# A fused attention, mixture-of-experts and squared-ReLU kernel: the cost rules by which its attention stage is put in order

## The chip, the cores and the metric

The kernel runs on one core of one Trainium2 chip. Its time is the device time of one execution in microseconds (us). TensorE does the matrix products, VectorE (DVE in the rows), ScalarE (ACT) and GpSimd (POOL) do elementwise work, SyncE (SP) issues most DMAs. Each engine carries out its instructions in the order in which the program lists them, and waits where a semaphore tells it to.

## The reference

Three layers follow one another. Sizes: batch 2, 8 heads, 576 positions, head size 64, so 1152 rows of 512; 4 experts with hidden size 1024; a last layer with hidden size 2048.

```python
# attention with a causal window of 128 and a slope per head
scores = scale * q @ k.T;  scores = where(0 <= rel < 128, scores + bias, -1e9)
attn = exp(scores - max);  attn = attn / (sum(attn) + 1e-9);  o = attn @ v
# every expert on every row, weighted
p = domain_probs / (sum(domain_probs) + 1e-9)
x = sum_e p[:, e] * (relu(o @ w1[e]) @ w2[e])
# last layer
h = relu(x @ w_in);  out = (h * h) @ w_out
```

All of it is float32. The kernel splits most operands into a rounded high part and a remainder ("h" and "l" in its names, as wh and wl, qh and ql, khl, xh and xl), and adds three products.

## The kernel before, in words

From the first microsecond to about 130 us the kernel does attention, and between its steps the first expert's rows: 24 "items" (three column chunks of the rows, 8 hidden blocks each), each a first product (L1031, for the first four L1819), a ReLU, and a second product (L1267, L1770). After that come the fourth chunk, the other experts and the last layer, whose order the program writes out directly.

The first stage's order isn't written by hand. The class `Plan` (L36 to L130) holds a list of tasks, each with the engines that may do it, with an assumed occupation and latency for each, the tasks that it depends on, and a due time. `Plan.run` repeats one step: it works out for each ready task the engine on which it would end first (a later engine of the task's list is taken only if it ends 0.3 us earlier: `OTHER`), finds the earliest start, and among the tasks that could start on that engine within 0.15 us of it (`LOOK`) emits the one with the earliest due time. So the plan fixes which engine does a task and the order of instructions on every engine; the chip's waits then keep the data right, whatever the real durations are.

The plan knows one kind of contention. Tasks marked `shared` (roundings and remainders that read and write SBUF: qh, ql, kh, kl, the first rows' xh and xl, and the weight parts wh and wl) are lengthened when they are put on VectorE while the last GpSimd task is still occupying GpSimd: by what is left of it, up to twice the task's own length. GpSimd tasks are never lengthened.

Attention goes through units (a batch, a pair of heads, up to two query tiles of 128). For each query tile `job_tasks` (L823) adds a chain: scores on TensorE (L868, or L852 for the last 64 rows), the mask on VectorE (L886, L884), bias and maximum on VectorE (L906, L899), exp on ScalarE with the sum (L915), the reciprocal on VectorE (L922, L926), the normalising multiplication `norm` (on GpSimd at L937; only the first tile of a batch, called raw, may also take VectorE, L931), the transposition on TensorE (L948), the copy out of PSUM (L519 or L521), and two triangular masks on GpSimd (L969). Then the product with v (L767) needs the masked tile. There are 32 such norm tasks outside the raw units: 24 with two squares of 128x128 and 8 with one.

The weights of the first expert come in 8 loads. Each becomes a wh (two halves, 128x512, L519 or L521) and a wl (two halves, L525) by `weight_parts` (L1705). The first four loads are used unconverted by the first four items, and their parts, needed again from the second chunk, are the last four in the list `parted` (places j = 4 to 7). For these, places 5 to 7 wait on the second product of the last item of the first chunk and on the remainders of the raw units (L1718).

Of the kernel before, what the change touches and what calls it, by code (L numbers as in the profile page):

```python
# [12 lines left out]
ACTF = mybir.ActivationFunctionType  # L13
# [16 lines left out]
class Buf:  # L30
# [3 lines left out]
    def __init__(self, kind):  # L34
        self.kind, self.users, self.end, self.tile = kind, 0, 0.0, None


class Plan:
# [6 lines left out]
    OTHER = 0.3  # L45
    COLD = 3.0
    WARM = 24.0

    def __init__(self, slots):
        self.tasks = []  # L50
        self.slots = slots
        self.held = {k: [] for k in slots}
        self.at = dict(PE=0.0, ACT=0.0, DVE=0.0, POOL=0.0, SP=0.0)
        self.pool_busy = (0.0, 0.0)

    def add(
        self, name, opts, fn, deps=(), takes=(), bufs=(), due=0.0, follow=(), cold=True,
        shared=False
    ):
        t = dict(  # L60
            name=name, opts=opts, fn=fn, deps=[d for d in deps if d], takes=list(takes),
            bufs=list(takes) + list(bufs), due=due, end=None, follow=[d for d in follow if d],
            cold=cold, shared=shared,
        )
        for b in t["bufs"]:
            b.users += 1
        self.tasks.append(t)
        return t
# [22 lines left out]
    def run(self, until=None):  # L91
        todo = self.tasks
        while todo and not (until and until()):
            cand = []
            for t in todo:
                r = self.ready(t)
                if r is None:
                    continue
                best = None
                for eng, occ, lat in t["opts"]:  # L100
                    start = max(self.at[eng], r)
                    if eng == "PE" and t["cold"] and start < self.COLD:
                        occ, lat = 1.7 * occ, lat + 0.7 * occ
                    if best is None or start + lat + self.OTHER < best[1] + best[3]:
                        best = (eng, start, occ, lat)
                cand.append((best, t))
            assert cand, [t["name"] for t in todo[:20]]
            first, _ = min(cand, key=lambda c: c[0][1])
            eng, start = first[0], first[1]
            (eng, start, occ, lat), t = min(  # L110
                (c for c in cand if c[0][0] == eng and c[0][1] <= start + self.LOOK),
                key=lambda c: c[1]["due"],
            )
            if eng == "DVE" and t["shared"] and self.pool_busy[1] > start:
                more = min(2.0 * occ, self.pool_busy[1] - start)
                occ, lat = occ + more, lat + more
            t["start"], t["end"] = start, start + lat
            self.gap = start - self.at[eng] if start < self.WARM else 0.0
            self.at[eng] = start + occ
            if eng == "POOL":  # L120
                self.pool_busy = (start, start + occ)
            for b in t["takes"]:
                self.held[b.kind].append(b)
            t["fn"](eng)
            for b in t["bufs"]:
                b.users -= 1
                b.end = max(b.end, t["end"])
            todo.remove(t)
# [3 lines left out]
def kernel(  # L132
# [14 lines left out]
    nc = tc.nc  # L147
# [12 lines left out]
    FTQ = FT // NQ  # L160
# [28 lines left out]
    def w_src(e, g, k):  # L189
        if k == 0:  # L190
            return w1s[e][0][:, g * FQ:(g + 1) * FQ].rearrange("(k p) f -> p k f", p=P), KT, FQ
        return w1s[e][1][g * FQ:(g + 1) * FQ, :].rearrange("(k p) d -> p k d", p=P), FTQ, DM
# [14 lines left out]
    def w_tile(shape, dtype, name):  # L207
        i = free.pop(0)
        return wbuf[i].tile(shape, dtype, tag=f"wb{i}", name=name), i
# [321 lines left out]
    def dve(n, lat=0.05):  # L531
        return ("DVE", 0.15 + 0.00105 * n, 0.15 + 0.00105 * n + lat)
# [4 lines left out]
    def pe(us):  # L537
        return ("PE", us, us + 0.25)
# [283 lines left out]
    def job_tasks(u, i, t, add, b_, end, ready, G, q0, k0, pos, wide):  # L822
# [5 lines left out]
        raw = t == 0  # L828
# [4 lines left out]
        rows, squares = (2 * n, 1) if twin else (n, G)  # L833
        s = {k: Buf(k) for k in ("sc", "ts", "st", "tp")}
        m = n if raw else P
# [5 lines left out]
        def stage(name, opts, fn, lag, **kw):  # L841
            mine[name] = add(key + name, opts, fn, due=end - lag - later, follow=[last.get(name)], **kw)
            return mine[name]
# [84 lines left out]
        def norm(eng):  # L928
            ts, st = s["ts"].tile, s["st"].tile
            if eng == "DVE":  # L930
                nc.vector.tensor_tensor(  # L931
                    out=ts[0:rows], in0=ts[0:rows],
                    in1=st[0:rows, 3, 0:squares].unsqueeze(2).to_broadcast([rows, squares, m]), op=ALU.mult,
                )
                return
            for g in range(squares):
                nc.gpsimd.tensor_scalar(  # L937
                    out=ts[0:rows, g, :], in0=ts[0:rows, g, :], scalar1=st[0:rows, 3, g:g + 1],
                    scalar2=1.0, op0=ALU.mult, op1=ALU.mult,
                )  # L940
# [34 lines left out]
        if twin:  # L975
            if "last" not in task:
                task["last"] = plan.add(
                    "last", [("POOL", 2.2, 2.3)], build_last, due=70.0,
                    deps=[task["bias", x, False] for x in range(NP)],
                )  # L980
            tb.append(task["last"])
        us = G * (0.25 if raw else 2 * max(0.107, w * 0.00047))
        tsc = stage("sc", [pe(us)], scores, 7.4, deps=ready,
                    takes=[s["sc"]],
                    bufs=[b_[k] for k in (() if raw else ("qh", "ql", "khl"))])
        if not raw:
            us = 0.15 + 0.00105 * G * n
            tsc = stage("jo", [("DVE", us, us + 0.05)], join, 6.8, deps=[tsc, tb[-1] if twin else t_keep], bufs=[s["sc"]])
        us = G * (0.215 if raw else 0.16 + 0.001 * m)
        tmx = stage("mx", [("DVE", us, us + 0.1)], top, 9.5 if raw else 6.4,  # L990
                    deps=[tsc] + tb, takes=[s["ts"], s["st"]], bufs=[s["sc"]])
        tex = stage("ex", [("ACT", squares * (0.30 + 0.00078 * m), squares * (0.30 + 0.00078 * m) + 0.1)], exp,
                    7.5 if raw else 5.3, deps=[tmx], bufs=[s["ts"], s["st"]])
        tin = stage("in", [("DVE", 0.33, 0.38)], inv, 3.8, deps=[tex], bufs=[s["st"]])
        us = squares * (0.44 if raw else 0.24 + 0.00085 * m)
        tno = stage("no", [("POOL", us, us + 0.05)] + [dve(G * m)] * raw,
                    norm, 3.4, deps=[tin], bufs=[s["ts"], s["st"]])
        ttp = stage("tp", [pe(squares * 0.108)], turn, 2.4, deps=[tno, task["ident"]],
                    takes=[s["tp"]], bufs=[s["ts"]])
        thi = stage("hi", [act(G * n), dve(G * n)], hi, 2.0, deps=[ttp],  # L1000
                    takes=[b_["pt"]] if i == 0 else [], bufs=[s["tp"]] + ([b_["pt"]] if i else []))
        if raw:
            return [thi]
        us = 0.2 + 0.00085 * G * n
        tow = stage("ow", [("POOL", us, us + 0.05)], lambda eng: part(True), 1.6, deps=[thi],
                    bufs=[b_["pt"]])
        tbe = stage("be", [("POOL", us, us + 0.05)], lambda eng: part(False), 1.4, deps=[tow],
                    bufs=[b_["pt"]])
# [425 lines left out]
    PER = 2 * NQ  # L1434
# [191 lines left out]
    for c in range(NP):  # L1626
        for own in (True, False):
# [3 lines left out]
                deps=[t_rel if own else t_join],  # L1631
# [28 lines left out]
    for u in range(len(units)):  # L1660
        if u < NP:
            unit_tasks(u, [14.0 + 2.0 * u])
        else:
            end = 38.0 + 5.5 * (u - NP)
# [4 lines left out]
    RAW1, RAW2 = 4, 4  # L1669
# [16 lines left out]
    def weight_parts(i):  # L1686
        e, g, k = order[i]
        _, nk, nf = w_src(e, g, k)
        parts = (w1t, w2t)[k]
        n = nk // 2  # L1690
        t = wtask["load", i]
        raw = FTQ * g < (RAW1, RAW2)[k]
        later = T0 + (T1 if raw else 0.0) + ITEM * (FTQ * g + (LAG if k else 0))

        def hi(eng, h):
            if h == 0:
                parts[e, g] = [w_tile([P, nk, nf], F32R, name) for name in ("wh", "wl")]
            ks = slice(h * n, (h + 1) * n)
            rounded(eng, parts[e, g][0][0][:, ks, :], wtask["raw", i][:, ks, :])

        def lo(eng, h):
            ks = slice(h * n, (h + 1) * n)
            (wh, _), (wl, _) = parts[e, g]
            rest(eng, wl[:, ks, :], wtask["raw", i][:, ks, :], wh[:, ks, :])
            if h == 1:  # L1705
                ready.add(i)
                if raw:
                    raw_done(i)
                else:
                    free.append(raws.pop(i)[0][1])  # L1710

        m = n * nf

        j = parted.index(i)
        room_ = [task["pv", NP - 1]] if j else []
        if j > 1:
            room_ += [wtask["lo", parted[j - 2], 1], wtask.get(("used", parted[j - 2]))]
        if raw and j > PER - (RAW1 + RAW2) // FTQ:  # L1718
            room_ += [itask["g2", FT - 1]] + [task["evl", u] for u in range(NP)]
        for h in range(2):  # L1720
            a = wtask["hi", i, h] = plan.add(
                f"wh{i}.{h}", [act(m), dve(m)], lambda eng, h=h: hi(eng, h),
                shared=True, deps=[t] + room_, due=later - 4.0 + h,
                follow=[wtask.get(("hi", i, 0))],
            )
            wtask["lo", i, h] = plan.add(
                f"wlo{i}.{h}", [gps(m), dve(m)], lambda eng, h=h: lo(eng, h),
                shared=True, deps=[a], due=later - 3.0 + h, follow=[wtask.get(("lo", i, 0))],
            )
# [163 lines left out]
    for i in range(PER):  # L1893
        weight_load(i)
    t_pt = plan.add("pt", [("SP", 0.6, 6.0)], lambda eng: nc.sync.dma_start(
        out=pt, in_=probs.rearrange("(t p) e -> p t e", p=P)
# [41 lines left out]
    for it, (e, ch, f, two) in list(enumerate(items))[N1:]:  # L1938
# [4 lines left out]
        g = f if two else f // FTQ  # L1943
# [66 lines left out]
```

## Time and profile before

| what | value |
|---|---|
| time, median of 3 runs | 647.51 us (647.49 to 647.77) |
| the profiled execution | 648.88 us |
| its span, first to last instruction | 646.9 us |
| TensorE busy in the span | 636.7 us (98%) |
| mean granted clock of TensorE | 0.997 |

The span is what the profile's rows lie in; the execution adds 2.0 us around it. TensorE's rows are pipelined: a row's length is its latency, and the steps between the starts of rows say how fast they go.

### The profile page before, as it was taken

The page shows a single profiled execution, that of the slowest core. Times are in us where ns is not written, and L with a number is a line of the kernel's source. Part 1 is how long each engine was busy: PE and PEld are TensorE (multiplying, and loading weights), DVE is VectorE, ACT ScalarE, POOL GpSimd, SP SyncE. Part 2 cuts the span into 40 slices and gives each one's busy share as a digit, 9 for nine tenths or more (in the row PEclk, how much of TensorE's full clock was granted, in tenths as well). Part 3 has the DMA queues.
Part 4 walks back from the last instruction along what each step waited for, and adds up shares of the span by engine and source line. Part 5 has one row for each costly group of instructions (what it writes and reads, how often), then busy time and mean ns, then how long its engine had stood idle before and what let it go on. Part 6 is the DMA issues. An engine that isn't in the chain of part 4 may idle for free.

```text
span 646.9 us, 11077 instructions
## 1 busy us (share of the span) xinstructions
PE 636.7 (98%) x3929; PEld 570.4 (88%) x3929; DVE 467.4 (72%) x1019; ACT 295.4 (46%) x744; POOL 393.0 (61%) x520
## 2 busy tenths in 40 slices
PE   9999999999999999999999999999999999999997
PEld 8767888899889999899899899899989899898996
DVE  6867967358887877876876876857777667767553
ACT  6867855334444444434434344346554543343230
POOL 2698977339784564565556546247786685665521
PEclk9989999999999999999999999999999999999999
DMA  9953341124125254354443443421114223001012
GB/s 231 275 144 84 81 106 47 39 93 131 34 65 163 82 143 151 93 157 126 119 142 114 130 131 115 130 83 66 33 41 157 81 83 114 16 2 50 1 65 82
DMA packets 46983, 64.70 MB, mean 100 GB/s; under 512 B 6480, under 2 KB 29264, under 8 KB 46928
## 3 DMA queue, kind: packets, MB, share of 16 engines
q1 hardware_dynamic: 35520, 39.48, 20.8%
q10 hardware_dynamic: 11408, 24.51, 12.9%
q8 instruction: 31, 0.51, 0.3%
q14 instruction: 24, 0.20, 0.1%
HBM read 53.23 MB, written 10.75 MB: 99 GB/s over the span
## 4 chain that ended last, share of the span: by engine, by line
PE 94%; POOL 3%; ACT 1%; issue 1%; DMA 0%; DVE 0%; POOLq 0%
PE yacc L1241 38%; PE hps L1150 35%; PE hps L1031 6%; PE yacc L1267 6%; PE sc L868 2%; PE xps L767 1%; PE tp L948 1%; PE hps L1819 1%; POOL ts L937 1%; PE sc L549 1%; POOL pt L969 1%; PE yacc L1770 1%; PE xtp L1333 1%; POOL ql L525 1%; ACT ts L915 0%
## 5 line engine op out<-in xcount | busy, mean ns | idle before, releaser
L1241 PE MATMUL yacc<-wh,hmem 128*128 128x512 f32 x716 | 227.8, 390 | 0.0
L1241 PEld LDWEIGHTS yacc<-wh,hmem 128*128 128x128 f32 x716 | 134.4, 188 | 27.1
L1241 PE MATMUL yacc<-wl,hmem 128*128 128x512 f32 x358 | 139.6, 390 | 0.0
L525 POOL TENSOR_TENSOR wl<-wraw,wh 128x256 fp32r<-128x256 f32 (+1 forms) x80 | 74.7, 958 | 40.8 <-ACT wh L458 29.1
L525 POOL TENSOR_TENSOR hmem<-c,hmem 128x320 fp32r<-128x320 f32 (+1 forms) x64 | 59.2, 943 | 60.3 <-ACT hmem L1181 60.3
L525 POOL TENSOR_TENSOR ls<-wsum,hs 128x256 fp32r<-128x256 f32 x77 | 61.5, 825 | 54.3 <-ACT hs L403 53.6
L1165 DVE TENSOR_TENSOR u<-hps,p 128x256 f32<-128x256 f32 (+1 forms) x80 | 36.4, 455 | 65.2 <-PE hps L1150 63.3
L1161 ACT ACTIVATE p<-hps 128x256 f32<-128x256 f32 (+1 forms) x80 | 32.8, 410 | 108.1 <-PE hps L1150 108.0
L1241 PEld LDWEIGHTS yacc<-wl,hmem 128*128 128x128 f32 x358 | 67.3, 188 | 12.5
L525 POOL TENSOR_TENSOR la<-wraw,ha 128x256 fp32r<-128x256 f32 x54 | 48.6, 919 | 16.8 <-ACT ha L389 16.8
L296 DVE SCALAR_TENSOR_TENSOR wconv<-wraw,wconv 128x512 int32<-128x512 int32 x64 | 57.6, 899 | 1.3
L1185 ACT ACTIVATE hmem<-c 128x256 fp32r<-128x256 f32 (+1 forms) x72 | 31.3, 445 | 53.4 <-DVE c L1165 51.8
L1186 DVE SCALAR_TENSOR_TENSOR hmem<-c,hmem 128x256 fp32r<-128x256 f32 (+1 forms) x72 | 43.3, 623 | 14.0 <-ACT hmem L1185 12.7
L1181 ACT ACTIVATE hmem<-c 128x320 fp32r<-128x320 f32 (+1 forms) x64 | 27.3, 446 | 52.3 <-DVE c L1175 33.5
L1150 PE MATMUL hps<-ht,ls 128*128 128x320 f32 (+1 forms) x160 | 47.5, 297 | 1.3 <-POOL ls L525 1.3
L1150 PE MATMUL hps<-xh,hs 128*128 128x320 f32 (+1 forms) x160 | 47.6, 297 | 0.0
L1150 PE MATMUL hps<-ht,hs 128*128 128x320 f32 (+1 forms) x160 | 47.5, 297 | 0.0
L1150 PE MATMUL hps<-xl,hs 128*128 128x320 f32 (+1 forms) x160 | 47.4, 296 | 0.0
L1150 PE MATMUL hps<-xh,la 128*128 128x320 f32 (+1 forms) x160 | 47.4, 296 | 0.0
L1150 PE MATMUL hps<-lt,hs 128*128 128x320 f32 (+1 forms) x160 | 47.3, 296 | 0.0
L1150 PE MATMUL hps<-xl,ha 128*128 128x320 f32 (+1 forms) x160 | 47.3, 296 | 0.0
L1150 PE MATMUL hps<-xh,ls 128*128 128x320 f32 (+1 forms) x160 | 47.3, 296 | 0.0
(162 smaller groups left out, 1643.6 us busy)
## 6 DMA issues: line engine op xcount, KB each, us to landing
wraw<-in_w_dram SPq DMA_DIRECT2D x32, 512.0 KB, 3.9
wraw<-in_w_out_dram ACTq DMA_DIRECT2D x16, 512.0 KB, 3.9
w<-wconv ACTq DMA_DIRECT2D x32, 256.0 KB, 4.1
wraw<-w SPq DMA_DIRECT2D x16, 512.0 KB, 3.8
wraw<-in_w_in_dram ACTq DMA_DIRECT2D x14, 512.0 KB, 4.1
rq<-in_qT_dram SPq DMA_DIRECT2D x8, 256.0 KB, 7.4
out_dram<-y SPq DMA_DIRECT2D x7, 256.0 KB, 2.1
rk<-in_kT_dram SPq DMA_DIRECT2D x8, 192.0 KB, 4.9
```

The costliest lines, as they stand in the source:

```text
L296: nc.vector.scalar_tensor_tensor(out=ai, in0=raw[j][:, :, part], scalar=amount, in1=ai, op0=op, op1=ALU.bitwise_or,)
L525: e.tensor_tensor(out=out, in0=in0, in1=f32(in1), op=ALU.subtract)
L868: nc.tensor.matmul(out=sc[0:n, g, :], lhsT=ql[:, qs], rhs=b_["khl"].tile[:, g, j0:j0 + w], start=(ql is b_["qh"].tile), stop=(ql is b_["ql ...
L1031: nc.tensor.matmul(out=ps, lhsT=l_[:, k, cs], rhs=r_[:, k, cols], start=(k == 0 and r_ is xh and l_ is wh and not second), stop=(k == KT - ...
L1150: nc.tensor.matmul(out=ps, lhsT=a[l_][:, k, :], rhs=b[r_][:, k, :], start=start and k == 0 and l_ == r_, stop=stop and k == 1 and l_ == 1, ...
L1161: nc.scalar.activation(out=out, in_=x, func=ACTF.Copy)
L1165: nc.vector.tensor_tensor(out=out, in0=x, in1=y, op=ALU.add)
L1181: nc.scalar.activation(out=hh, in_=r, func=ACTF.Copy)
L1185: nc.scalar.activation(out=hh, in_=src, func=ACTF.Relu)
L1186: nc.vector.scalar_tensor_tensor(out=hl, in0=src, scalar=0.0, in1=f32(hh), op0=ALU.max, op1=ALU.subtract)
L1241: nc.tensor.matmul(out=y, lhsT=l_[:, ns], rhs=r_[:, fo, cols], start=(first and fo == 0 and j == 0), stop=(last and fo == FTQ - 1 and j == 2),
L1267: nc.tensor.matmul(out=y, lhsT=l_[:, ns], rhs=r_[:, fo, :], start=(first and j == 0), stop=(last and j == 2),)
```

## The change

`Plan` keeps for each of GpSimd and VectorE the last task that may hold what both use: on GpSimd every task, on VectorE a `shared` one. When a GpSimd task starts while the kept VectorE task is still running, 0.65 (`HELD`) of what is left of it is added to the GpSimd task. When a `shared` VectorE task starts while the kept GpSimd task is running, 0.3 (`SLOWED`) of the overlap is added to the VectorE task, and 0.65 of the overlap to the GpSimd task, whose end and whose engine's free time move out. The choice of an engine is still made before anything is added.

The norm tasks outside the raw units get ScalarE as a second engine, assumed at 0.22 us a square, as one activation a square (Copy, with the reciprocal as the scale).

Of the parts of the raw weights, only the last place (j = 7) still waits on the last item of the first chunk; places 5 and 6 don't.

```diff
+    HELD = 0.65
+    SLOWED = 0.3
...
-        self.pool_busy = (0.0, 0.0)
+        self.port = dict(POOL=None, DVE=None)
...
-            if eng == "DVE" and t["shared"] and self.pool_busy[1] > start:
-                more = min(2.0 * occ, self.pool_busy[1] - start)
+            other = self.port["POOL" if eng == "DVE" else "DVE"]
+            if other and (eng == "POOL" or eng == "DVE" and t["shared"]):
+                end = other["start"] + other["occ"]
+                if eng == "POOL":
+                    more = self.HELD * max(end - start, 0.0)
+                else:
+                    both = min(occ, max(end - start, 0.0))
+                    more = self.SLOWED * both
+                    other["occ"] += self.HELD * both
+                    other["end"] += self.HELD * both
+                    self.at["POOL"] = max(self.at["POOL"], other["start"] + other["occ"])
                 occ, lat = occ + more, lat + more
-            t["start"], t["end"] = start, start + lat
+            t["start"], t["end"], t["occ"] = start, start + lat, occ
...
-            if eng == "POOL":
-                self.pool_busy = (start, start + occ)
+            if eng == "POOL" or eng == "DVE" and t["shared"]:
+                self.port[eng] = t
...
+            if eng == "ACT":
+                for g in range(squares):
+                    nc.scalar.activation(
+                        out=ts[0:rows, g, :], in_=ts[0:rows, g, :], func=ACTF.Copy,
+                        scale=st[0:rows, 3, g:g + 1],
+                    )
+                return
...
-        tno = stage("no", [("POOL", us, us + 0.05)] + [dve(G * m)] * raw,
-                    norm, 3.4, deps=[tin], bufs=[s["ts"], s["st"]])
+        us_act = squares * 0.22
+        tno = stage("no", [("POOL", us, us + 0.05)] + (
+            [dve(G * m)] if raw else [("ACT", us_act, us_act + 0.1)]
+        ), norm, 3.4, deps=[tin], bufs=[s["ts"], s["st"]])
...
-        if raw and j > PER - (RAW1 + RAW2) // FTQ:
+        if raw and j > PER - (RAW1 + RAW2) // FTQ + 2:
```

## Rows read from the trace of the kernel before

**Rows 1.** The page's first part: busy us, share of the span, instructions.
```profile
PE 636.7 (98%) x3929; PEld 570.4 (88%) x3929; DVE 467.4 (72%) x1019; ACT 295.4 (46%) x744; POOL 393.0 (61%) x520
```
**Rows 2.** Busy time by stage: stretch, its length, engines' busy us (instructions), granted clock, DMA.
```profile
24.00:95.00 71.00, 67.31 (x470) 54.89 (x469) 53.85 (x197) 50.68 (x159) 64.26 (x105) 0.98 0.49 127
95.00:130.00 35.00, 34.89 (x276) 31.39 (x276) 18.18 (x78) 15.71 (x53) 17.90 (x40) 1.00 0.18 53
130.00:647.00 517.00, 512.00 (x2983) 464.14 (x2981) 378.00 (x667) 211.61 (x473) 304.20 (x359) 1.00 0.30 93
```
**Rows 3.** TensorE's waits, 17 to 130 us: us in total, times, longest.
```profile
PE tp L948 <- POOL ts L937: 3.5, 5, 1.0
```
**Rows 4.** The view by stage again, in stretches of 1 us.
```profile
42.00:43.00 1.00, 0.11 (x1) 0.11 (x1) 0.93 (x4) 0.50 (x2) 1.00 (x2) 1.00 0.97 273
43.00:44.00 1.00, 0.44 (x3) 0.25 (x3) 1.00 (x2) 0.00 (x0) 1.00 (x2) 0.92 0.51 176
44.00:45.00 1.00, 1.00 (x6) 1.00 (x6) 0.17 (x1) 0.73 (x2) 1.00 (x2) 0.50 0.82 228
47.00:48.00 1.00, 1.00 (x7) 0.79 (x6) 0.43 (x1) 0.42 (x2) 0.34 (x1) 0.87 0.31 103
```
**Rows 5.** Timeline of GpSimd: start, us, instruction.
```profile
33.43 2.01 POOL L525 TENSOR_TENSOR ql<-rq,qh 128x512 fp32r<-128x512 f32 x1
36.10 1.28 POOL L525 TENSOR_TENSOR wl<-wraw,wh 128x512 fp32r<-128x512 f32 x1
40.52 1.26 POOL L525 TENSOR_TENSOR wl<-wraw,wh 128x512 fp32r<-128x512 f32 x1
41.77 1.96 POOL L937 TENSOR_SCALAR ts<-ts,st 128x128 f32<-128x128 f32 x2
79.86 1.93 POOL L525 TENSOR_TENSOR wl<-wraw,wh 128x512 fp32r<-128x512 f32 x1
81.74 0.88 POOL L969 TENSOR_SCALAR_AFFINE_SELECT pt<-pt 128x256 f32<-128x256 f32 x2
82.61 0.37 POOL L937 TENSOR_SCALAR ts<-ts,st 128x128 f32<-128x128 f32 x1
```
**Rows 6.** Timeline of VectorE.
```profile
33.33 0.95 DVE L525 TENSOR_TENSOR khl<-rk,khl 64x768 fp32r<-64x768 f32 x1
36.53 1.41 DVE L525 TENSOR_TENSOR wl<-wraw,wh 128x512 fp32r<-128x512 f32 x1
40.34 0.17 DVE L926 RECIPROCAL st<-st 128x2 f32<-128x2 f32 x1
40.95 1.65 DVE L525 TENSOR_TENSOR khl<-rk,khl 64x768 fp32r<-64x768 f32 x1
42.90 0.67 DVE L525 TENSOR_TENSOR wl<-wraw,wh 128x512 fp32r<-128x512 f32 x1
```
**Rows 7.** Groups of instructions, shapes apart, 24 to 130 us: count, busy us, mean ns.
```profile
L937 POOL TENSOR_SCALAR ts<-ts,st 128x128 f32<-128x128 f32 x56 | 25.1, 459 | 10.3 <-ACT khl L519 4.9 <-DVE st L926 2.4 <-ACT pt L519 1.7
L969 POOL TENSOR_SCALAR_AFFINE_SELECT pt<-pt 128x256 f32<-128x256 f32 x48 | 23.4, 491 | 5.1 <-ACT pt L519 3.3
L915 ACT ACTIVATE ts<-ts,st 128x128 f32<-128x128 f32 x54 | 21.1, 393 | 7.1 <-DVE st L906 5.8 <-DVE st L899 1.3
L525 POOL TENSOR_TENSOR wl<-wraw,wh 128x512 fp32r<-128x512 f32 x8 | 11.2, 1405 | 0.1
L525 POOL TENSOR_TENSOR ql<-rq,qh 128x512 fp32r<-128x512 f32 x5 | 7.9, 1576 | 0.0
L525 DVE TENSOR_TENSOR wl<-wraw,wh 128x512 fp32r<-128x512 f32 x8 | 7.7, 974 | 0.1
L525 DVE TENSOR_TENSOR khl<-rk,khl 64x768 fp32r<-64x768 f32 x6 | 6.7, 1113 | 0.2
L519 ACT ACTIVATE pt<-tp 128x128 f32<-128x128 f32 x8 | 2.2, 277 | 5.4 <-PE tp L948 5.3
```
**Rows 8.** Timeline of ScalarE: the raw weights' first roundings.
```profile
65.59 1.14 ACT L519 ACTIVATE wh<-wraw 128x512 fp32r<-128x512 f32 x2
```

## The prediction

> **What bounds the kernel now.** I read the page's shares first. TensorE is busy 636.7 of 646.9 us [rows 1], so only the 10.2 that TensorE loses can move the time, and whatever its clock takes. The table of busy time by stage says where [rows 2]. After 130 us it misses 5.0 of 517, in a part whose order the plan doesn't make; from 95 to 130 it misses 0.11. From 24 to 95 it misses 71.00 - 67.31 = 3.69, so that 1.4 is left for the time before 24, the loads and the raw units' chain. In the stage from 24 to 95 GpSimd is the busiest helper, 64.26 of 71 us (91%), against VectorE's 53.85 (76%) and ScalarE's 50.68 (71%).
>
> TensorE's own waits name the cause: transpositions wait on GpSimd's norm five times, 3.5 us in all [rows 3], nearly all of the 3.69. The first of these waits has an aftermath. TensorE is busy 0.11 in the 42nd microsecond and 0.44 in the next; then the granted clock, 0.92 in that one, is 0.50 (the 1.2 GHz level of the two) in the three from 44 to 47, of which one stands here, and 0.87 in the next [rows 4]. At full clock these five would have taken 0.08 + 3 x 0.50 + 0.13 = 1.71 us less. What the change can win in this stage is 3.5 + 1.7 = 5.2 us.
>
> Why the norm is late is in the timelines. At 40.51 its reciprocal is ready (40.34 + 0.17) [rows 6], but GpSimd is in a weight remainder until 41.78, and the two squares of the norm then take 1.96 us, where an undisturbed square takes 0.37; and that one, at 82.61, comes only after a remainder of 1.93 and a mask pair of 0.88 [rows 5].
>
> **The change, part by part.**
>
> *Contention counted both ways.* The rows show that whichever of the two engines begins first goes on undisturbed, and the other is held. At 33.33 VectorE begins a khl of 0.95 us; GpSimd's ql at 33.43 takes 2.01. At 36.10 GpSimd begins a wl of the same size and takes 1.28; VectorE's wl at 36.53 takes 1.41 instead of the 0.67 of 42.90 [rows 5, 6]. The old plan books the second case and misses the first. How much it misses, by means against undisturbed ones: norms 56 x (459 - 370) = 5.0 us, masks 48 x (491 - 440) = 2.4 (440 is half of the pair of 0.88), wl and ql of 128x512 8 x (1405 - 1280) + 5 x (1576 - 1280) = 2.5 [rows 5, 7]. GpSimd is held 9.9 us, and none of it is planned. VectorE is held 8 x (974 - 670) + 6 x (1113 - 950) = 3.4 us [rows 6, 7], and that was planned.
>
> The new booking adds 0.65 of the rest to a GpSimd task that comes second, so 0.35 of it stays unbooked; and 0.3 to a VectorE task that comes second, so 0.7 stays unbooked, while 0.65 is charged to a GpSimd task that in the rows isn't held at all (36.10). With half of the norms gone from GpSimd (below), the held time there falls by 2.5 us, to 7.4. Unbooked is then 0.35 x 7.4 + 0.7 x 3.4 = 2.6 + 2.4 = 5.0 us, against 9.9. I price lateness by what it cost TensorE: 5.2 us lost for 9.9 unbooked, 0.53 each. So 5.0 x 0.53 = 2.65 us is lost again. The bounds: none of it reaches TensorE (0), or all of it does, with one more stretch at the half clock (5.0 + 1.7 = 6.7). I stay at the measured ratio, because the same chain, order rule and buffers turn lateness into waits as before.
>
> The Trainium skill, "SBUF — State Buffer", section "Who interferes with whom", puts it as a lock: the one that issues first keeps the shared pair for its whole instruction, and the other blocks fully. The four rows above agree. By it the factors 0.65 and 0.3 are wrong in each single case, and far too mild for VectorE; the last rival below is where that leads.
>
> *Norms on ScalarE.* No row shows this operation. Nearest below is the copy of a 128x128 out of PSUM, 277 ns, nearest above the exp of a 128x128 in SBUF, 393 ns, with a bias and a sum [rows 7]. Two squares end to end so take 0.55 to 0.79 us; I take 0.32 a square, nearer to the copy, as no sum is written. GpSimd takes 0.74 undisturbed, and 1.96 at worst. ScalarE is chosen where it ends 0.3 us before GpSimd: by the plan's numbers (0.54 against 0.75) where GpSimd comes free 0.1 us later than ScalarE. At a load of 91% that is often; I say 16 of 32 tasks, 28 squares. About three quarters of the tasks lie before 95 us. So there GpSimd sheds 0.75 x 25.1 / 2 = 9.4 us [rows 7] and falls from 64.3 to 55 of 71, and ScalarE gains 0.75 x 28 x 0.32 = 6.7 and goes to 57. At the first wait ScalarE could start the norm when the reciprocal ends, 1.26 us before GpSimd did, and isn't held by VectorE; the others go likewise. So the 5.2 us goes: this is the gross gain. Queued behind a norm on ScalarE are the next exp, the copies that free the transposition's banks, and the items' ReLU. If a norm stands there waiting for VectorE's reciprocal, all these wait, and behind them TensorE; this cost is in the 2.65, with VectorE's unbooked 2.4.
>
> *Raw weights' parts.* The roundings held back by the wait begin at 65.59 [rows 8]. Free of it, those of places 5 and 6, four roundings of 0.57 and four remainders (1.28 each on GpSimd or 0.67 on VectorE, undisturbed), fall some 5 to 15 us earlier, wherever an engine has nothing due sooner. TensorE's waits of 17 to 130 us name none of these tasks [rows 3], so the relief is worth 0. The cover is gone if a remainder gets in front of a norm: 1.28 us a time, bound 0 to 2.6 (two of the four). I take 0, as a norm can now go to ScalarE. No step that moves issues a DMA; SP's loads keep their order by `follow`.
>
> *Start and end.* In the raw chain the norms keep their two engines, and no booking changes until the first `shared` task is on VectorE: 0. After 95 TensorE is never short of work (0.11 idle), so a gain before it is passed on.
>
> **The sum.** -5.2 + 2.65 + 0 = -2.5 us. On the profiled execution 648.88 - 2.5 = 646.4, with a span of 644.4. The median of the runs stands 1.37 below the profiled execution, so 647.5 - 2.5 = 645.0 us.
>
> **The rivals.**
>
> *Everything goes* (0.12). No lateness reaches TensorE: -5.2, and a little more where small gaps close, 642.0. For it: all waits of this stage have one releaser. Against it: single bookings stay wrong in both directions.
>
> *Nothing measurable* (0.23). ScalarE, itself at 71%, is seldom early enough, or the waits move from the norm to another step of the same chain on GpSimd (the masks are as long in sum, 23.4 us [rows 7]): 5.2 lost as before, 647.5.
>
> *Slower: norms on ScalarE wait for VectorE* (0.20). The place is 30 to 80 us. VectorE's reciprocals stand behind remainders that are now booked at 0.3 of a hold and take all of it, as khl at 40.95, 1.65 us for 0.95 [rows 6]. ScalarE then waits at its head, with exp, copies and ReLUs behind. Price: all of the 5.0 unbooked and a further stretch at the half clock, 6.7 - 5.2 = +1.5, 649.0; with two such stretches 650.7. It decides from the point where the new waits reach 5.2, so that each unbooked microsecond has to reach TensorE, where half of them do now. For it speaks that ScalarE would be the busiest helper, at 57 of 71; against it, that TensorE has no wait on ScalarE or VectorE in this stage [rows 3].
>
> **How the numbers follow.** The forecast, 645.0, has 0.45, with a range of its own of 643.3 to 646.2. A difference under 0.2%, 1.3 us, can't be told from none. Faster: 0.45 + 0.12 = 0.57; within: 0.23; slower: 0.20. The range that is to hold 8 in 10 leaves half of the first rival and half of the last outside: 642.2 to 649.0.
>
> **What would show it.** Right: ScalarE has rows of the norm, some 28 squares of 0.3 us; GpSimd's busy time from 24 to 95 us falls to near 55; TensorE's waits on L937 fall from 3.5 to under 1; no stretch of 0.50 stands in the clock after 17 us. Wrong: the rows on ScalarE are few; TensorE's waits name ScalarE or a reciprocal instead; a stretch of 0.50 stands elsewhere; or TensorE's idle time after 130 us, 5.0 now, has changed, which no step here explains.

## The result, and the profile after

The changed kernel takes 641.26 us (median of 4 runs, 641.12 to 641.43) against 647.51; the ratio is 0.9902, with an interval of 0.9887 to 0.9916. That is 6.25 us less, where 2.5 were forecast, and 0.9 below the low end of the range. The profiled execution takes 641.43 us, 7.45 less than that of before.

Of the 61 executions of before that ran beside the experiments, 42 have a mean granted clock of 1.000 (median 647.7 us, 647.2 to 648.9) and 19 one of 0.997 (median 649.2, 648.4 to 649.4); the profiled one, 648.88, has 0.997 and belongs with the 19, and the median above belongs with the 42.

The page after, first part (columns as in [rows 1]):

```profile
PE 633.3 (99%) x3929; PEld 569.2 (89%) x3929; DVE 470.3 (74%) x1023; ACT 299.3 (47%) x763; POOL 384.3 (60%) x497
```

Busy time by stage after, as in [rows 2]:

```profile
24.00:95.00 71.00, 71.00 (x523) 60.27 (x522) 62.30 (x225) 59.32 (x193) 59.30 (x90) 1.00 0.52 136
95.00:130.00 35.00, 35.00 (x261) 31.26 (x261) 15.87 (x61) 11.74 (x41) 13.03 (x32) 1.00 0.18 57
130.00:639.70 509.70, 504.80 (x2946) 457.79 (x2945) 374.83 (x662) 210.97 (x472) 305.33 (x359) 1.00 0.30 93
```

From 24 to 95 us TensorE is busy 71.00 of 71.00, where it missed 3.69; the granted clock is 1.00 there, against 0.98; after 130 it misses 4.9, as before (5.0, of which 0.1 lies behind the end of the span). From 17 to 130 us the view names no wait any more, so the 3.5 us of [rows 3] are gone. Groups of 24 to 130 us after, as in [rows 7]:

```profile
L987 POOL TENSOR_SCALAR_AFFINE_SELECT pt<-pt 128x256 f32<-128x256 f32 x48 | 24.3, 511 | 2.7 <-ACT pt L530 0.8
L955 POOL TENSOR_SCALAR ts<-ts,st 128x128 f32<-128x128 f32 x35 | 15.1, 441 | 15.3 <-DVE st L937 6.4 <-ACT khl L530 4.9 <-ACT pt L530 2.3
L536 POOL TENSOR_TENSOR ql<-rq,qh 128x512 fp32r<-128x512 f32 x6 | 9.8, 1631 | 0.8 <-ACT qh L530 0.8
L536 POOL TENSOR_TENSOR wl<-wraw,wh 128x512 fp32r<-128x512 f32 x7 | 9.5, 1358 | 0.1
L536 DVE TENSOR_TENSOR wl<-wraw,wh 128x512 fp32r<-128x512 f32 x9 | 9.4, 1052 | 0.1
```

Of the 56 norm squares, 35 stay on GpSimd. The other 21 are these, by source line (minimum, median, maximum in ns; first and last start):

```profile
L949 ACT ACTIVATE ts<-ts,st x21: 387/391/408, 27.0 to 85.6; 128x128 f32<-128x128 f32 x21
```

The contention on GpSimd has hardly gone. By the prediction's own method GpSimd is held 35 x (441 - 370) + 48 x (511 - 440) + 7 x (1358 - 1280) + 6 x (1631 - 1280) ns = 2.5 + 3.4 + 0.5 + 2.1 = 8.5 us (9.9 before). What is gone is the idle time of TensorE that went with it. The timeline after, where the situation of 40 to 44 us in [rows 5, 6] comes again:

```profile
40.91 0.17 DVE L937 RECIPROCAL st<-st 128x2 f32<-128x2 f32 x1
41.51 0.95 DVE L536 TENSOR_TENSOR khl<-rk,khl 64x768 fp32r<-64x768 f32 x1
41.52 0.69 ACT L949 ACTIVATE ts<-ts,st 128x128 f32<-128x128 f32 x2
41.70 1.91 POOL L536 TENSOR_TENSOR ql<-rq,qh 128x512 fp32r<-128x512 f32 x1 [0.17 <-ACT qh L530]
42.49 1.67 DVE L536 TENSOR_TENSOR wl<-wraw,wh 128x512 fp32r<-128x512 f32 x1
42.74 0.38 PE L966 MATMUL tp<-ident,ts 128*128 128x128 f32 x2
```

GpSimd's ql is held (1.91) and then VectorE's wl (1.67); the norm runs on ScalarE beside the khl and the ql, ends at 42.21, and its transposition comes at 42.74, after other work of TensorE.

How much a wait had cost is read from the starts. TensorE in before, at three of its five waits:

```profile
41.43 0.44 PE L948 MATMUL tp<-ident,ts 128*128 128x128 f32 x2
42.89 0.33 PE L948 MATMUL tp<-ident,ts 128*128 128x128 f32 x1 [1.02 <-POOL ts L937]
43.78 0.45 PE L948 MATMUL tp<-ident,ts 128*128 128x128 f32 x1 [0.56 <-POOL ts L937]
...
81.71 0.27 PE L852 MATMUL sc<-khl,ql 128*128 128x192 f32 x1
83.03 0.33 PE L948 MATMUL tp<-ident,ts 128*128 128x128 f32 x1 [1.04 <-POOL ts L937]
...
128.88 0.33 PE L1031 MATMUL hps<-xh,wh 128*128 128x384 f32 x1
```

The view names 1.02, 0.56 and 1.04 us. But the row before a wait still shows 0.27 to 0.33 us of latency in which nothing new starts. From start to start the third is 83.03 - 81.71 = 1.32, less the 0.11 that such a step takes undisturbed: 1.2 us. The second is 0.89 less 0.11, 0.78 instead of 0.56. The four largest waits together are 4.1 us by their starts, where the view names 3.35. The last row is the first product with 384 columns, where the fourth chunk's work begins; after, it is this one:

```profile
121.48 0.33 PE L1051 MATMUL hps<-xh,wh 128*128 128x384 f32 x1
```

That is 7.40 us earlier, which is nearly the whole difference of the profiled executions (7.45). 1.7 of it is the stretch at half clock [rows 4]. Of the other 5.7, 4.1 are those four waits; the rest, the fifth wait and smaller gaps, is not followed row by row.

### The profile page after: what moved, and what is told of

It reads as the page before. It is cut to its first block, busy times and chain, and to the rows that moved or that the text cites. A ratio compares the mean times of both kernels' runs of the same rounds, so it can differ in the third digit from the quotient of the medians.

```text
span 639.7 us, 11060 instructions
## 1 busy us (share of the span) xinstructions
PE 633.3 (99%) x3929; PEld 569.2 (89%) x3929; DVE 470.3 (74%) x1023; ACT 299.3 (47%) x763; POOL 384.3 (60%) x497
## 4 chain that ended last, share of the span: by engine, by line
PE 98%; ACT 1%; DVE 0%; POOL 0%; issue 0%; POOLq 0%
PE yacc L1261 38%; PE hps L1170 35%; PE hps L1051 7%; PE yacc L1287 7%; PE xps L778 2%; PE sc L879 2%; PE tp L966 1%; PE hps L1839 1%; PE yacc L1790 1%; PE sc L560 1%; PE xtp L1353 1%; PE sc L863 1%; ACT ts L926 1%; PE sc L871 0%; PE xps L764 0%; PE ylast L1261 0%
```

## The experiments

Each ratio is to before, run again beside the experiment (medians of 647.8 to 648.4), with its 95% interval. The theories in words: by theory B the gain is the booking, since a plan that knows GpSimd's pace puts TensorE's other work in the gaps; by N it is the norm's engine; by P the weights' parts; by L it is luck, since any edit draws another order. "Idle" is what TensorE lacks from 24 to 95 us (3.69 before).

### Each part alone, and three norms moved by hand

The booking alone (the diff of `Plan`, nothing else):

> The new booking of contention alone, on the kernel before (norms stay on GpSimd, the parts wait as before). Before is 647.5 us, the changed kernel 641.3. Theory N (the norm's second engine carries the gain): GpSimd stays at 90% of the stage from 24 to 95 us and the norm keeps coming late, so 645.5 to 648.5. Theory B (the booking carries it: a plan that knows that GpSimd is held puts its tasks in an order that fits): 641 to 643.5, with TensorE's waits on the norm under 1 us. Theory L (luck: any other list order moves some 3 us either way): anything from 642 to 650.

642.42 us, 0.9910 (0.9892 to 0.9928), in the range of theory B; the interval overlaps that of the whole change. Its stage and its only wait from 17 to 130 us, then its groups and timeline:

```profile
24.00:95.00 71.00, 70.42 (x516) 58.96 (x515) 62.69 (x226) 54.09 (x168) 61.92 (x104) 1.00 0.51 133
```

```profile
PE tp L959 <- POOL ql L536: 0.5, 1, 0.5
```

```profile
L948 POOL TENSOR_SCALAR ts<-ts,st 128x128 f32<-128x128 f32 x56 | 27.4, 502 | 12.6 <-ACT khl L530 4.9 <-DVE st L937 4.3 <-ACT pt L530 1.7
L536 POOL TENSOR_TENSOR wl<-wraw,wh 128x512 fp32r<-128x512 f32 x4 | 5.5, 1368 | 0.1
L536 DVE TENSOR_TENSOR wl<-wraw,wh 128x512 fp32r<-128x512 f32 x12 | 11.1, 929 | 0.0
```

```profile
44.65 0.71 POOL L948 TENSOR_SCALAR ts<-ts,st 128x128 f32<-128x128 f32 x2
46.97 0.38 PE L959 MATMUL tp<-ident,ts 128*128 128x128 f32 x2
50.89 1.15 POOL L948 TENSOR_SCALAR ts<-ts,st 128x128 f32<-128x128 f32 x2 [0.30 <-DVE st L917]
54.02 0.41 PE L959 MATMUL tp<-ident,ts 128*128 128x128 f32 x2 [0.48 <-POOL ql L536]
```

All 56 squares are on GpSimd, and they are held longer than before (502 ns against 459 in [rows 7]). Yet the view names no wait for a norm: one ends at 45.36 and its transposition comes at 46.97, another ends at 52.04 and its transposition comes at 54.02, after a wait that the view puts to the ql behind the norm, not to the norm. In before a norm ended at 43.73 (41.77 + 1.96) and TensorE was already waiting. Paired in order, 13 of the 56 squares in before are followed by their transposition within 0.1 us of their end, so that TensorE was there already or nearly so; with the booking 5 are. Four weight remainders went from GpSimd (8 to 4) to VectorE (8 to 12).

ScalarE's option alone (the diff of `norm` and `tno`):

> ScalarE as the norm's second engine alone, with the old booking and the old wait of the parts. Theory N: 641 to 643.5, TensorE's waits on the norm gone. Theory B: the plan still thinks GpSimd undisturbed, so it sends few norms to ScalarE and the order is late as before: 645 to 648.5. Theory L: anything from 642 to 650.

645.30, 0.9957 (0.9943 to 0.9971), in theory B's range; idle 2.10. Its two largest waits, and one of its three whole microseconds at the half clock:

```profile
PE tp L955 <- POOL ts L944: 1.6, 1, 1.6
PE hps L1828 <- ACT hfirst L1762: 1.1, 1, 1.1
```

```profile
46.00:47.00 1.00, 1.00 (x2) 0.34 (x1) 0.64 (x2) 1.00 (x4) 0.84 (x1) 0.50 0.65 205
```

The option takes away part of the waits and leaves the cause: a norm that stays on GpSimd is still late. This profiled execution, with a half-clock stretch, took 647.21, 1.9 above its own median; the other five executions have a mean granted clock of 1.000, so the stretch isn't in every execution of a kernel.

The parts alone (`+ 2` in the condition on `raw`):

> Only the wait of two of the raw weights' parts taken away. Theories N and B: no change of note, 646 to 649, as TensorE waited for no part of a weight; up to 650 where a remainder gets ahead of a norm. Theory P (the early parts take the load from 65 to 80 us and carry the gain): 641 to 644.

646.66, 0.9973 (0.9963 to 0.9983), in the range of theories N and B; idle 3.28, and the norm is waited for as before, 2.7 us in three waits:

```profile
PE tp L948 <- POOL ts L937: 2.7, 3, 1.1
PE sc L868 <- DVE khl L525: 0.6, 1, 0.6
```

Before's plan as it was, but three of the norms emitted on ScalarE whatever the plan says:

```diff
+            if not raw:
+                state["norms"] = state.get("norms", 0) + 1
+                if state["norms"] in (7, 9, 18):
...
+                        nc.scalar.activation(
...
+                    return
```

> The plan of before, untouched, but the three norms on which TensorE waits longest (the 7th, 9th and 18th outside the raw units) are done by ScalarE in the place that the plan gave them on GpSimd. Theory N: the three waits go, 3.5 us by their rows and about 4.9 by the steps between TensorE's starts, and with them the half clock of 44 to 47 us, 1.7: 641 to 643.5. Theory B: the lateness of GpSimd is still there and the next task of the chain takes the wait: 644 to 647.

645.33, 0.9955 (0.9940 to 0.9970), in theory B's range and not in N's; idle 1.02. The larger of the two groups of waits that are left, and one of its places:

```profile
PE tp L958 <- POOL ts L947: 0.5, 2, 0.3
```

```profile
81.68 0.39 PE L1277 MATMUL yacc<-wh,hmem 128*128 128x512 f32 x1
82.37 0.67 PE L958 MATMUL tp<-ident,ts 128*128 128x128 f32 x2 [0.30 <-POOL ts L947]
```

The order on every engine's queue is before's, apart from these three norms, so TensorE's steps can be compared one by one. The four steps at the moved norms are 3.9 us shorter, but six later ones, of over 0.1 us each, are 1.6 us longer: the step shown is 0.69 us, where the same one in before takes 0.23 (85.78 to 86.01). So the named waits were real, but with the old order part of them comes back at the next norms, and taking them away is worth 2.2 us.

### Leaving one part out

After without the booking (`Plan` of before):

> The changed kernel with the old booking: norms may go to ScalarE, the parts wait on fewer items. Alone these were 645.3 and 646.7 us, the booking alone 642.4, before 648.0. Theory B (the booking carries most): 644 to 646, with a wait of TensorE on the norm left. Theory N (norm and parts together are enough): 641 to 642.5.

643.97, 0.9935 (0.9920 to 0.9950), at the lower end of theory B's range; idle 2.02, with 1.9 us of waits on the norm left.

After without ScalarE's option (`tno` of before):

> The changed kernel with the norms kept on GpSimd: new booking and fewer waits of the parts. Theory B: 641 to 642.5, no worse than the booking alone (642.4). Theory N: GpSimd, near 90% busy, shows waits again: 643 to 645.

642.28, 0.9917 (0.9893 to 0.9941), in theory B's range; idle 0.84.

After without the parts (`+ 2` taken out):

> The changed kernel with the old wait of the raw weights' parts: booking and norms. All three 641.3, booking alone 642.4, booking and parts 642.3. Theory B: 641 to 642.3, the parts being worth under 1 us once the norm's waits are gone. Theory P: 642.5 to 644.

643.08, 0.9925 (0.9911 to 0.9940), in theory P's range and not in B's; idle 1.28.

Against 647.5 the booking brings 5.1 alone, the option 2.2 and the parts 0.9: 8.2 in sum, where all three bring 6.25. On top of the other two they bring 2.7, 1.0 and 1.8. Without the booking the other two bring 3.5 together. The three edits partly replace one another, and the booking by itself comes within 1.2 us of the whole. It is the largest part, by itself and on top of the others, but each figure stands for one order, and the draws below move the time by up to 3.4 us.

### Which feature of the booking

The lock in full: who comes second gets all that is left of the other, who came first nothing.

```diff
-                if eng == "POOL":
-                    more = self.HELD * max(end - start, 0.0)
-                else:
...
+                more = max(end - start, 0.0)
```

On before's other parts:

> On the kernel before, a booking as the single rows read: the task that comes second is lengthened by all that is left of the first, on either engine, and the first by nothing. Booking alone with 0.65 and 0.3 gave 642.4. Theory B1 (what counts is that each task is booked as it runs): as good or better, 640.5 to 642.5. Theory B2 (what counts is only that GpSimd is charged for its holds on the average): the same within 1 us, 641.5 to 643.5. Theory L (luck of the order): anything from 642 to 650.

645.23, 0.9956 (0.9941 to 0.9971); idle 2.03. In the changed kernel:

> The changed kernel with the booking as the single rows read (the second waits for all that is left of the first, the first loses nothing). On the kernel before this booking gave 645.2 where 0.65 and 0.3 gave 642.4. If that gap is the booking's: 642.5 to 645. If it was the draw of one order: 640.5 to 643, beside the changed kernel's 641.3.

643.48, 0.9930 (0.9915 to 0.9945); idle 1.52. The first is slower than both forms of theory B had it (640.5 to 643.5), the second lies where the gap would be the booking's. I had thought the exact rule better or as good, and in both kernels it came out 2.2 to 2.8 us slower, which is no more than a draw moves.

The traces show why "in full" isn't exact either. VectorE's subtractions are held by more than 0.3 us only while a long subtraction runs on GpSimd, as the wl at 42.49 above. Beside a square or a mask they lose up to 0.28 us, while the square that starts second loses most of the other's time. The Trainium skill, "SBUF — State Buffer", section "Who interferes with whom", gives the lock to one whole instruction at a time; these rows agree, and a task of two short instructions so holds the lock shortly, and can lose it between them, as I read the two squares of 1.96 us in [rows 5]. A booking by instruction (a norm or mask holds nothing, and a norm is moved back by a whole VectorE task):

```diff
+                left = max(end - start, 0.0)
+                short = other["name"][:1] == "j" and other["name"][2:4] in ("no", "ow", "be")
+                more = left
+                if eng == "DVE" and short:
+                    more = 0.0
+                    if other["name"][2:4] == "no" and left > 0.35:
+                        other["occ"] += occ
...
```

On before's other parts, and in the changed kernel:

> On the kernel before, a booking by instruction, as the single rows of four traces read: VectorE is held (for the rest) only by GpSimd's long subtractions; against a norm or a mask it isn't held, and a pair of norms loses VectorE's whole time between its squares; a GpSimd task that comes second loses the rest. The simple lock gave 645.2, 0.65 and 0.3 gave 642.4. Theory B1 (the nearer to the rows, the better): 640.5 to 642.5. Theory O (enough that norms are expected late, the details don't matter): 642 to 644.5. If the order drawn matters more than the booking: 644.5 to 648.

> The changed kernel (norms on ScalarE too, fewer waits of the parts) with the booking by instruction in place of 0.65 and 0.3. That booking alone gave 644.2 and left no wait on the norm, only some on VectorE's khl and wl; the changed kernel is 641.3 to 642.9 in three draws. If the details of the booking don't matter once GpSimd is charged: 641 to 643, a version as good as the changed kernel. If the mixed factors fit better by their own merit: 643 to 645.

644.24, 0.9942 (0.9927 to 0.9957), idle 2.19; and 642.40, 0.9913 (0.9898 to 0.9928), idle 1.10. In these two draws it is no better than the mean factors: the first lies in theory O's range and not in B1's, the second where the details don't matter. The largest waits of the first are on VectorE and ScalarE now:

```profile
PE sc L880 <- DVE khl L537: 0.9, 2, 0.7
PE hps L1831 <- ACT hfirst L1765: 0.5, 1, 0.5
PE hps L1043 <- DVE wl L537: 0.5, 1, 0.5
```

No contention in the plan beyond before's, but each GpSimd task booked 15% longer:

```diff
+                    if eng == "POOL":
+                        occ, lat = 1.15 * occ, lat + 0.15 * occ
```

The 15% is rough: the 9.9 us were held over 24 to 130 us, where GpSimd is busy 82.2.

> On the kernel before, with its old rule for VectorE: every GpSimd task is booked 15% longer (9.9 us held of 64.3 busy), whenever it runs. Theory B2 (the average charge is enough): 641.5 to 643.5. Theory B1 (the hold has to be booked where it falls): 644.5 to 647. Theory L: anything from 642 to 650.

643.72, 0.9931 (0.9916 to 0.9946), between the ranges of theories B2 and B1, nearer to B2's. Its stage and its groups:

```profile
24.00:95.00 71.00, 70.07 (x508) 58.37 (x508) 55.54 (x213) 53.24 (x169) 66.99 (x110) 1.00 0.50 130
```

```profile
L939 POOL TENSOR_SCALAR ts<-ts,st 128x128 f32<-128x128 f32 x56 | 27.6, 506 | 9.5 <-ACT khl L521 4.9 <-DVE st L928 1.6 <-ACT pt L521 1.6
L527 POOL TENSOR_TENSOR wl<-wraw,wh 128x512 fp32r<-128x512 f32 x9 | 12.6, 1396 | 0.0
```

GpSimd is busier than before in this stage (66.99 of 71, 64.26 before; 81.9 against 82.2 over 24 to 130, as more of the work now falls before 95), keeps all norms and has one remainder more, and its norms take 506 ns in the mean (459 before). TensorE loses 0.93 instead of 3.69. So neither a lighter GpSimd nor less contention is needed: a plan that knows GpSimd to be slower is enough for 3.8 us.

The norm's result expected 0.9 us later, with nothing charged to GpSimd (the theory that only TensorE's order counts: it need only come later for a norm):

```diff
-        tno = stage("no", [("POOL", us, us + 0.05)] + [dve(G * m)] * raw,
+        tno = stage("no", [("POOL", us, us + (0.05 if raw else 0.95))] + [dve(G * m)] * raw,
```

> The kernel before, its booking, engines and waits untouched; only the plan takes the norm's result to come 0.9 us later than its work ends (GpSimd stays free as early as before). Theory O (the booking works through TensorE's order: a plan that expects the norm late puts other products ahead of the transposition, and a norm as late as ever then costs nothing): 642 to 645, TensorE's waits on the norm under 1 us while the norms end as long after their reciprocals as before. Theory G (GpSimd has to be relieved or its tasks reordered): 646 to 649.

647.78, 0.9997 (0.9987 to 1.0007), in theory G's range; idle 4.02.

```profile
PE tp L948 <- POOL ts L937: 1.7, 4, 0.7
PE yacc L1267 <- ACT wh L519: 1.3, 1, 1.3
```

The waits on the norm halve and others appear. In this draw theory O missed by far. Of the plans that keep the norms on GpSimd and before's parts, only those gained more than 2 us that charge GpSimd's own time, which moves all that is queued there.

### How much is the draw of an order

A list schedule turns any small edit into another order. Two of before's own constants, neither to do with contention:

```diff
-    LOOK = 0.15
+    LOOK = 0.12
```

> The kernel before with nothing of the change; only the window within which the plan picks the earliest due time goes from 0.15 to 0.12 us. Theory L (the order of before is one unlucky draw, and any other draw is some 3 us better): 643 to 646. Theory B (without the booking the waits on GpSimd stay): 646.5 to 650.

646.43, 0.9975 (0.9966 to 0.9985), between the two ranges; idle 2.25.

```diff
-    OTHER = 0.3
+    OTHER = 0.25
```

> The kernel before with nothing of the change; only the lead that a second engine needs goes from 0.30 to 0.25 us. Theory L: 643 to 646. Theory B: 646.5 to 650.

650.74 (648.69 to 653.16), 1.0042 (1.0023 to 1.0060), beyond both ranges on B's side; idle 5.21, most of its waits on the norm again. Five of the ten executions have a granted clock of 0.997, and the other five a median of 649.5:

```profile
PE tp L948 <- POOL ts L937: 3.6, 3, 2.2
```

The same two edits on the changed kernel, and `LOOK` on the booking by instruction alone:

> The changed kernel with the same 0.12 us window. Theory B (the booking makes orders that fit, whichever order it draws): 640.5 to 643. Theory L (641.3 is a lucky draw): 643 to 646.

> The changed kernel with a lead of 0.25 us for a second engine instead of 0.30, the alteration that took the kernel before from 647.8 to 650.7. Theory B (with the booking, orders fit whichever is drawn): 640.5 to 643. Theory L: 643 to 646.

> The booking by instruction on the kernel before, once more with the plan's window at 0.12 us instead of 0.15, that is another draw of its order. If 644.2 was the draw: anywhere from 641.5 to 644.5. If this booking is worse than 0.65 and 0.3 (642.4): 643.5 to 646, again with waits on VectorE.

641.43, 0.9901 (0.9886 to 0.9917), idle 0.00; 642.93, 0.9924 (0.9910 to 0.9939), idle 1.00; and 640.86, 0.9890 (0.9872 to 0.9907). The first two lie in theory B's range; the last is below its own range (641.5 to 644.5) and the lowest time of all, with GpSimd keeping every norm and before's parts:

```profile
24.00:95.00 71.00, 70.53 (x522) 59.94 (x521) 63.19 (x228) 54.13 (x172) 60.39 (x103) 1.00 0.50 128
```

Its interval overlaps that of after, so it isn't shown to beat it; the same rule with the other `LOOK` gave 644.24, 3.4 more.

Taken together: without ScalarE's option and with before's parts, four plans that don't charge GpSimd take 646.4, 647.5, 647.8 and 650.7 us (mean 648.1), and five that do, by four rules, 640.9, 642.4, 643.7, 644.2 and 645.2 (mean 643.3). The sets don't overlap. The charge is worth 4.8 us in the mean (4.5 if 649.5, at full clock, stands for the 650.7), and a constant that says nothing of contention moved the time by 0.2 to 3.4 us under one and the same rule. The option with the parts adds, under three rules each, 642.42 - 641.26 = 1.2, 645.23 - 643.48 = 1.8 and 644.24 - 642.40 = 1.8; with one draw each that isn't shown apart from luck, and 640.86, without them, is below 642.40, with them.

## Why the prediction was wrong

**Where it was right.** The gain lies between 24 and 95 us, and TensorE's waits on the norm there are gone (under 1 was forecast). No half clock stands after 17 us. The idle time after 130 us is unchanged. GpSimd fell to 59.30 (55 forecast) and ScalarE rose to 59.32 (57), in a stage that now holds more of the work (523 products of TensorE, 470 before).

**The step that failed: "So 5.0 x 0.53 = 2.65 us is lost again".** I took lateness left unbooked to reach TensorE at the old ratio, "because the same chain, order rule and buffers turn lateness into waits as before". GpSimd is held 8.5 us after and 9.9 before, and TensorE shows no idle time; in the flat plan the norms are held longer than before, and a quarter of the idle time is left. A plan doesn't have to predict each hold. Measured by idle time, the term is 0; idle time isn't all (the plan with 0.47 of it took 640.86), but the measured time lies below the 642.0 of a sum with nothing lost again. Where the order stays, the premise holds: with three norms moved by hand 1.6 of 3.9 us came back. The order doesn't stay when the booking changes. I read it so (the pairs of norms and transpositions show it, 13 close ones in before, 5 with the booking; in the flat plan there are still 10, and no run isolates it): once GpSimd's mean pace is about right, TensorE, which has other work at hand, mostly comes for a norm after it is ready.

**What was held.** The 9.9 us are a little low, and so are the 8.5: an undisturbed mask takes 0.41 us by the median of its rows, not 0.44, which adds 1.6 to both. They also cover 24 to 130 us, where the 5.2 that I divided by them were lost before 95.

**The size of the waits.** I took the view's 3.5 us. By starts the four largest are 4.1, and with the small gaps 5.7 went. Over before, after and the 18 kernels run, the median time rises by 1.7 us with each us of idle time from 24 to 95 us (a line through the 20 pairs, scatter 0.8 us; the three norms moved by hand lie 2.3 above it); 3.69 x 1.7 = 6.3, the measured gain of the medians, though the line is drawn through these two kernels too.

**The half clock, counted on both sides.** The 1.71 us stood in the gain, and the 1.37 by which the median lies under the profiled execution was taken off afterwards as a constant. The executions of before with a granted clock of 0.997 take 1.5 us more in the median than those with 1.000, and the ScalarE kernel's one execution with a stretch 1.9 more. So the stretch is most of the 1.37, and the median execution doesn't have it. On the median the sum should have been the waits, no clock and nothing given back; with the 5.7 read afterwards that is 641.8, against 641.26.

**The norms on ScalarE.** 21 squares, not 28, at 391 ns a row, not 320: the upper bound was right for a row, though a pair end to end takes 0.69 us, near the 0.64 that I took. It mattered little, since the booking alone removes nearly all waits; I had hung the whole gross gain on this part and treated the booking as what gives some of it back. That was the wrong way round.

**The parts.** Forecast at 0; alone they brought 0.9, and 1.8 on top of the other two edits, which is within what a draw of the order moves.

**The rivals.** "Everything goes", 642.0, is nearest to what came, at 0.12. "Slower" named ScalarE waiting for VectorE, and TensorE behind it: TensorE has no wait on ScalarE after, and of its waits with the option alone 1.1 us is on an item's result (hfirst) and 0.2 on a norm; the longest on a norm of ScalarE in any run is 0.5 (the full lock in the changed kernel).

**What stays open.** By which single moves the charge works (TensorE's order, or the remainders that go to VectorE) isn't settled: the flat plan gains without the second, expecting only the norm late gained nothing in its one draw. Nor is what makes one draw better than another.

## What to carry to other kernels

Where a planner writes the order, book the busiest helper at the pace it really runs, by the mean of its rows under load; a rough factor got 3.8 of the 6.25 us here. Price a stall by the step from start to start, not by the idle figure beside it. And before an edit of a planner is credited with a microsecond, run a few draws of the order with and without it.

## What the runs showed of the hardware

The half clock came in some executions only of one and the same program: 1.7 us of it in a profile of before [rows 4], a granted clock of 0.997 and 1.5 us more in 19 of 61 executions of before, and 1.9 us between a profiled execution and the median of another kernel. A scaled copy of 128x128 in SBUF on ScalarE took 391 ns, as long as the exp of the same size (393), while a pair end to end took 0.68 to 0.70, less than GpSimd's 0.71 to 0.72 undisturbed.
